# A fourth Strassen unit in token tile 2 of a pooled-attention and SiLU-MLP kernel, with VectorE and ScalarE work moved between tiles

## The chip, the cores and the metric

The kernel runs on one core of a Trainium2 chip. The metric is the device time of one execution in microseconds (us), lower is better. The kernel before takes 277.86 us, the median of 4 runs (277.79 to 278.11). In the profile's words, PE is TensorE (matmuls) and PEld its weight loads, DVE is VectorE, ACT is ScalarE, POOL is GpSimd, and SP is SyncE, which here only issues stores.

## The reference, cut to what matters

Eight batches of 576 tokens, eight heads of 64 features. Keys and values are averaged over groups of 8 tokens, so each head attends from 576 queries to 72 pooled keys. The result, 4608 tokens by 512 features, goes through a two-layer network with SiLU between. All arguments are float32; the kernel multiplies in bfloat16 and accumulates in float32.

```python
k_p = k.reshape(B, H, Sp, pool, D).mean(axis=3)
v_p = v.reshape(B, H, Sp, pool, D).mean(axis=3)
scores = scale * np.matmul(q, k_p.transpose(0, 1, 3, 2))
scores = scores - np.max(scores, axis=-1, keepdims=True)
attn = np.exp(scores)
attn = attn / (np.sum(attn, axis=-1, keepdims=True) + 1e-09)
x = (attn @ v_p), heads side by side      # [4608, 512]
h = x @ w_in                              # w_in [512, 2048]
g = h * (1.0 / (1.0 + np.exp(-h)))
out = (g @ w_out).astype(np.float32)      # w_out [2048, 512]
```

## The kernel before, in words

**Tiles.** The 4608 tokens are cut into nine token tiles of 512 (t = 0 to 8). A tile has an up stage (x @ w_in and SiLU, into the tile h_T, 16 groups of 128 hidden features) and a down stage (h_T @ w_out, into o_sb and out). While tile t runs, the attention of batch t + 1 is worked in between: q is transposed on VectorE (L164), scores go through exponentials on ScalarE (L353), denominators through a logarithm and an exponential (L372, L373), and numerators are scaled into xT on VectorE (L398). The batch is handled in three thirds, called visits. Pooling of k and v is done by accumulating DMAs from GpSimd's queue (L185, L189) and additions on GpSimd (L195, L198), from batch 3 on; batches 0 to 2 are pooled with VectorE sums (L268, L272).

**Units.** A plain group multiplies one group of 128 hidden features with four matmuls of 512 columns (L547). A unit is a 2 x 2 block product done with seven products in place of eight, after Strassen and Winograd. It covers four groups: seven products of four matmuls of 256 columns each (L493). The products need sums of input blocks (x_sum, L449, per tile) and sums of weight blocks (w_sum1, L442, made once), and their results are joined in PSUM and in the tiles r_sb, rr_sb, t_sb and c_sb (L511, L514, L517, L526, L529), with SiLU at L501. Units are named y = 0, 1, 2, 3, or A, B, C, E in a text program. The down stage is one such block product over the whole tile: seven products of 16 matmuls, from sums of hidden blocks (h_sum, L615, per tile) and of w_out blocks (w_sum, L633, made once).

**Which tile does what.** Tile 0 is all plain. Tile 1 has two units and eight plain groups, tile 2 three units and four plain groups, and tiles 3 to 8 four units. The constant `T4 = 3` says from which tile on `run(t)` is used. Before it, the up stage is a list of items, and every other engine's work is a filler with a step number in the lists f_up and f_down; the fillers are issued when the step is reached, so these numbers set the order in each engine's queue. The up stage of tile 1 has 60 steps, the down stage 112; fillers with larger numbers follow at the end. From T4 on the order is one text, PROGRAM, whose tokens name products (C2, E6), hidden sums (h5h), parts of the down products (d40), attention steps (sc0, de1, nu0), the next tile's input sums (x3) and two subtractions (u1, u2). All engines work in order.

**The down stage, two forms.** `down_quarters` (L656 to L690; tiles 1 and 2) issues the products 2, 5, 1, 4, 3, 7, 6. Products 5, 3 and 6 share the PSUM bank Q, and product 3's result is copied out of it to o_sb[0] at L682 before product 6 adds to it. `down_stages` (L712 to L754; from T4 on) begins with 4 and 3 and keeps their sum in rr_sb, from which two results are then subtracted at L754 (tokens u1, u2): on GpSimd for t below 7, on VectorE for tiles 7 and 8.

**Weight sums.** The sums of units 0 and 1 are made in tile 0, those of unit 2 at the end of tile 1 (into space that k and v of batch 2 leave), those of unit 3 at the end of tile 2: three into the same space and two into the tile w_e. The last halves of two w_out sums (n = 4 and 7) are made in the down stage of tile 1.

Of the kernel before, what the change touches and what calls it, by code (L numbers as in the profile page):

```python
# [36 lines left out]
def kernel(  # L37
# [9 lines left out]
    nc = tc.nc  # L47
# [594 lines left out]
    def down_quarters(t, fillers, last=False):  # L642
        step = spread(fillers, 7 * 2 * KQ)
        ps = {
            n: ps_tile([128, 2, CQ], FP32, "mm", f"o_ps{n}") for n in "PQR"
        }
        bank = {2: "P", 5: "Q", 1: "R", 4: "P", 3: "Q", 7: "P", 6: "Q"}
        begun = set()
        r_sb, rr_sb, t_sb = r_sbs[0], rr_sbs[0], t_sbs[0]

        def product(n, k0, k1, cs=(0, 1)):
            b = bank[n]
            for kt in range(k0, k1):
                for c in cs:
                    next(step)
                    nc.tensor.matmul(  # L656
                        ps[b][:, c, :], lhsT=left(n, kt, c), rhs=W_OUT[n][:, kt, :],
                        start=b not in begun,
                        stop=kt == k1 - 1, skip_group_check=True,
                    )  # L660
                    begun.add(b)

        add, sub = ALU.add, ALU.subtract
        tt = nc.vector.tensor_tensor
        KA = KQ // 2
        product(2, KA, KQ)
        product(5, KA, KQ)
        product(2, 0, KA)
        nc.scalar.copy(r_sb, ps["P"])
        product(5, 0, KA)  # L670
        tt(out=rr_sb, in0=ps["Q"], in1=r_sb, op=add)
        for cc in ((0,), (1,)) if last else ((0, 1),):
            cs = slice(cc[0], cc[-1] + 1)
            product(1, 0, KQ, cc)
            tt(out=t_sb[:, cs], in0=ps["R"][:, cs], in1=rr_sb[:, cs], op=sub)
            product(4, 0, KQ, cc)
            nc.scalar.copy(o_sb[1][:, cs, LO], ps["P"][:, cs])
            tail = last and cc == (1,)
            if tail:
                store(t, 3, LO, (nc.gpsimd,))  # L680
            product(3, 0, KQ, cc)
            nc.vector.tensor_copy(out=o_sb[0][:, cs, HI], in_=ps["Q"][:, cs])  # L682
            if tail:
                store(t, 1, HI)
            product(7, 0, KQ, cc)
            tt(out=o_sb[0][:, cs, LO], in0=ps["P"][:, cs], in1=t_sb[:, cs], op=add)
            for c in cc:
                store(t, c, LO if tail else FULL, (nc.scalar if tail else nc.sync,))
            product(6, 0, KQ, cc)
            tt(out=o_sb[1][:, cs, HI], in0=ps["Q"][:, cs], in1=t_sb[:, cs], op=add)  # L690
            for c in cc:
                if tail:
                    store(t, 3, HI, both)
                else:
                    store(t, 2 + c, FULL, (nc.gpsimd if last else nc.sync,))
        for _ in step:
            pass


    def down_stages(t, last):  # L700
        ps = {}
        bank = {2: "P", 5: "Q", 1: "R", 4: "P", 3: "Q", 7: "P", 6: "Q"}
        begun = set()
        r_sb, rr_sb, t_sb = r_sbs[0], rr_sbs[0], t_sbs[0]
        add, sub = ALU.add, ALU.subtract
        tt = nc.vector.tensor_tensor

        def matmuls(n, k0, k1, cs=(0, 1)):
            b = bank[n]
            for kt in range(k0, k1):  # L710
                for c in cs:
                    nc.tensor.matmul(  # L712
                        ps[b][:, c, :], lhsT=left(n, kt, c), rhs=W_OUT[n][:, kt, :],
                        start=b not in begun,
                        stop=kt == k1 - 1, skip_group_check=True,
                    )
                    begun.add(b)

        def after(n, cc=(0, 1), tail=False):
            cs = slice(cc[0], cc[-1] + 1)  # L720
            if n == 4:
                nc.scalar.copy(r_sb, ps["P"])
            elif n == 3:
                tt(out=rr_sb, in0=ps["Q"], in1=r_sb, op=add)
            elif n == 2:
                nc.scalar.copy(o_sb[1][:, :, LO], ps["P"])  # L726
                if last:
                    store(t, 3, LO, (nc.gpsimd,))
            elif n == 5:
                copy = nc.scalar.copy if last else nc.vector.tensor_copy  # L730
                copy(out=o_sb[0][:, :, HI], in_=ps["Q"])
                if last:
                    store(t, 1, HI)
            elif n == 1:
                tt(out=t_sb[:, cs], in0=ps["R"][:, cs], in1=rr_sb[:, cs], op=add)
            elif n == 7:
                tt(out=o_sb[0][:, cs, LO], in0=ps["P"][:, cs], in1=t_sb[:, cs], op=add)
                for c in cc:
                    store(t, c, LO if tail else FULL, (nc.scalar if tail else nc.sync,))
            else:  # L740
                tt(out=o_sb[1][:, cs, HI], in0=ps["Q"][:, cs], in1=t_sb[:, cs], op=add)
                for c in cc:
                    if tail:
                        store(t, 3, HI, both)
                    else:
                        store(t, 2 + c, FULL, (nc.gpsimd if last else nc.sync,))

        def part_of(tok):
            if tok == "o":
                return after(6)  # L750
            n = int(tok[1])
            if tok[0] == "u":
                src = o_sb[1][:, :, LO] if n == 1 else o_sb[0][:, :, HI]
                (nc.gpsimd if t < B - 1 else nc.vector).tensor_tensor(  # L754
                    out=rr_sb, in0=rr_sb, in1=src, op=sub
                )
                return
            b = bank[n]
            if b not in ps:
                tag = f"mm{'PQR'.index(b)}"  # L760
                ps[b] = ps_tile([128, 2, CQ], FP32, tag, f"o_ps{b}")
            i = int(tok[2])
            k0 = 2 * i if n == 4 else 2 * (i ^ 2)
            matmuls(n, k0, k0 + 2)
            if i == 3 and n != 6:
                after(n)

        def columns(c):
            if not c:
                ps["R"] = ps_tile([128, 2, CQ], FP32, "mm2", "o_psR")  # L770
            for n in (1, 7, 6):
                matmuls(n, 0, KQ, (c,))
                after(n, (c,), c == 1)

        return part_of, columns
# [163 lines left out]
    def load_half_2(name, half):  # L939
        for i0, i1 in ((0, SA), (SA, SLOTS), (SLOTS, SLOTS + 1)):  # L940
            load_slots(nc.gpsimd, 2, name, i0, i1, half)

    THREE = (
        "A2 A5 g0 B2 A4 A1 A3 B5 C2 A7 B4 A6 Ah B1 B3 As C5 B7 C4 B6 Bh C1 C3 C7 Bs g1"
        " C6 Ch Cs g2 g3",
        "A2 A5 g0 A4 B2 A3 A1 B5 A7 C2 A6 B4 B3 B1 C5 Ah B7 As C4 Bh B6 C1 C3 C7 Bs g1"
        " C6 Ch Cs g2 g3",
    )
    visits = [third(n) for n in range(3)]
    T4 = 3  # L950
    for t in range(NT):
        a = t + 1
        if t >= T4:
# [11 lines left out]
            f_up += [(17, lambda: numerators(0, part(1, 1)))]  # L965
        else:
            G = lambda *gs: [(g, 0, NTT) for g in gs]
            if t == 1:
                items = (
                    G(12, 13, 14, 15) + [(0, "25143"), (1, "2"), (0, "7"), (1, "5")]  # L970
                    + [(0, "6h"), (1, "1")] + G(0) + [(1, "4"), (0, "s"), (1, "3")] + G(1)
                    + [(1, "7h6")] + G(2) + [(1, "s")] + G(3)
                )
            else:
                items = []
                for it in THREE[t // B].split():
                    items += [(("BCA".index(it[0])), it[1])] if it[0] in "ABC" else G(int(it[1]))
            if t == 1:
                for n in U_X:
                    f_up.append((0, lambda n=n: unit_x_sum(t, n)))  # L980
# [1 line left out]
                h_at = 50 if t == B else 54 if t > 1 else 45  # L982
                f_up.append((h_at, lambda n=n: hidden_sum(n, 4, 8)))
            f_up.append((56, lambda: hidden_sum(6, 4, 8)))
            for n, k0 in ((2, 0), (5, 0), (1, 4), (1, 0)):
                f_up.append((64, lambda n=n, k0=k0: hidden_sum(n, k0, k0 + 4)))
            f_down.append((33 if t > 1 else 44, lambda: hidden_sum(7, 0, 8)))
            f_down.append((71 if t < B else 50, lambda: hidden_sum(6, 0, 4)))
# [1 line left out]
        for n, t0, f_to, at, parts in (  # L990
            (1, 0, f_down, 16, (0, 2)), (3, 0, f_down, 30, (0, 2)),
            (1, 0, f_down, 46, (2, PW)), (3, 0, f_down, 50, (2, PW)),
            (6, 0, f_down, 8, (0, PW)), (4, 0, f_down, 12, (0, 2)),
            (7, 0, f_down, 14, (0, 2)), (4, 1, f_down, 20, (2, PW)), (7, 1, f_down, 52, (2, PW)),
        ):
            for i in range(*parts):
                if t == t0:
# [64 lines left out]
        if t == 1:  # L1062
            def unit_weight_tiles():
                k_w = big.tile([128, 4, 2, 256], BF16, tag="k_raw2", name="w_sum12")
                v_w = big.tile([128, 4, 2, 256], BF16, tag="v_raw2", name="w_sum12")
                w_sum1.append([k_w[:, i] for i in range(4)] + [v_w[:, 0]])
                w_sum1.append([v_w[:, 1 + i] for i in range(3)] + [w_e[:, i] for i in range(2)])

            f_down.append((72, unit_weight_tiles))
            for i, n in enumerate(U_W):  # L1070
                f_down.append((73 if i < 2 else 81, lambda n=n: unit_weight_sum(2, n)))
        if t == 2:
            for i, n in enumerate(U_W):
                f_down.append((76 + 2 * i, lambda n=n: unit_weight_sum(3, n)))
        if t != 1:
            moe_tables()
        if t == 0:
# [34 lines left out]
```

The softmax here doesn't subtract the row's maximum and nothing guards it: scores larger than these inputs give would overflow.

## Time and profile before

| what | value |
|---|---|
| median of 4 runs | 277.86 us |
| the profiled execution, time | 277.86 us |
| its span, first to last instruction | 276.0 us |
| busy: PE, DVE, ACT, POOL | 269.9, 243.5, 192.4, 111.5 us |
| TensorE clock granted | 1.00 |
| h_sum, 128x1024 (L615), 76 of them | 788 ns mean |
| weight sum, 128x512 (L442, w_in) | 414 ns mean |
| copy of o_psQ at L682 on VectorE | 686 ns mean |
| copy of o_psP at L677 on ScalarE | 586 ns mean |
| subtraction at L754 on GpSimd, 8 of them; on VectorE, 4 | 1779 ns; 684 ns mean |
| first matmul of tiles 1, 2, 3, 4 | 50.91, 80.72, 109.45, 137.80 us |

The span is what the trace covers; the time of the execution holds 1.86 us more. A timeline row gives the start in us, the length, the engine, the line, what is written and read, and in brackets the idle time of that engine just before and what ended it. A run of equal instructions is merged into one row with a count. Two instructions of one engine overlap a little: a single input sum of 128x512 takes 0.42 us, but two take 0.75. A matmul's end is modelled, so the time of a matmul is best read from the start of one to the start of the next. A few matmul records are missing from the trace, and PE is then shown idle for that time.

### The profile page before, as it was taken

The numbers are of one execution on the slowest core, as the hardware profiler recorded it, in microseconds if no ns is written. First come the engines' busy times: TensorE is split into PE (matmuls) and PEld (weight loads), VectorE is DVE, ScalarE is ACT, GpSimd is POOL, SyncE is SP. The second block draws the span as 40 slices with busy tenths as digits, with TensorE's granted clock in tenths as the row PEclk, the third lists the DMA queues.
The fourth block names the chain that finished last, engine by engine and source line by source line (L and its number), as shares of the span: only waits on it lengthen the run. The fifth ranks groups of instructions, "written<-read, shape, count | busy, mean of one in ns | idle before, by whom it ended". The sixth has DMA issues, their size and how long they took to land.

```text
span 276.0 us, 7362 instructions
## 1 busy us (share of the span) xinstructions
PE 269.9 (98%) x2923; PEld 209.1 (76%) x2933; DVE 243.5 (88%) x452; ACT 192.4 (70%) x374; POOL 111.5 (40%) x112
## 2 busy tenths in 40 slices
PE   8999999999999999999999999999999999999995
PEld 4448444576778678887888778877887788888884
DVE  4986778778998879998999999999999899998994
ACT  1688767468668976789777986798688868407730
POOL 8755116342148530964377326986550400000000
PEclk9999999999999999999999999999999999999999
DMA  7999999997659879558846844599620042005003
GB/s 211 278 244 257 205 312 200 243 181 126 147 68 211 228 110 162 147 160 124 135 119 163 148 75 125 140 152 134 135 57 2 2 103 53 0 13 144 1 26 128
DMA packets 31314, 37.73 MB, mean 137 GB/s; under 512 B 10352, under 2 KB 22256, under 8 KB 31280
## 3 DMA queue, kind: packets, MB, share of 16 engines
q0 software_dynamic: 23920, 27.03, 52.3%
q1 hardware_dynamic: 6928, 9.58, 12.6%
q10 hardware_dynamic: 432, 0.66, 0.6%
q8 instruction: 23, 0.38, 0.6%
q14 instruction: 11, 0.09, 0.1%
HBM read 36.70 MB, written 9.44 MB: 167 GB/s over the span
## 4 chain that ended last, share of the span: by engine, by line
PE 83%; DMA 14%; issue 1%; POOL 0%; DVE 0%; POOLq 0%
PE u_psP L493 14%; PE u_psQ L493 14%; PE o_psQ L712 12%; PE o_psP L712 12%; DMA w_in_sb<-in_moe_w_in_dram 7%; DMA w_out_sb<-in_moe_w_out_dram 6%; PE u_psR L493 5%; PE o_psR L712 4%; PE o_psQ L656 4%; PE o_psP L656 4%; PE hp_ps L547 4%; PE sc_ps L345 3%; PE nu_ps L389 3%; PE o_ps L582 2%; DMA q_bf<-in_q_dram 2%; PE den_ps L363 2%
## 5 line engine op out<-in xcount | busy, mean ns | idle before, releaser
L615 DVE TENSOR_TENSOR h_sum<-h_T 128x1024 bf16<-128x1024 bf16 (+1 forms) x78 | 58.9, 799 | 2.8 <-ACT h_T L501 1.6
L493 PEld LDWEIGHTS <-w_sum 128*128 128x128 bf16 x532 | 52.0, 98 | 7.2 <-issue 0.3
L712 PEld LDWEIGHTS <-h_sum 128*128 128x128 bf16 x480 | 45.8, 98 | 8.1 <-issue 2.5
L353 ACT ACTIVATE es<-sc_ps 72x384 bf16<-72x384 f32 (+1 forms) x100 | 39.1, 472 | 5.5 <-PE sc_ps L345 5.3
L501 ACT ACTIVATE h_T<-c_sb 128x512 bf16<-128x512 f32 x58 | 35.7, 630 | 6.2 <-DVE c_sb L529 3.6
L511 ACT COPY r_sb<-u_psP 128x512 f32<-128x512 f32 x29 | 17.0, 586 | 19.3 <-PE u_psP L493 19.2
L547 PE MATMUL hp_ps<-xT,w_in_sb 128*128 128x512 bf16 (+2 forms) x151 | 26.1, 317 | 0.3
L398 DVE TENSOR_TENSOR xT<-nu_ps,rec 128x384 bf16<-128x384 f32 (+1 forms) x50 | 23.9, 528 | 1.8 <-PE nu_ps L389 1.4
L493 PEld LDWEIGHTS <-w_in_sb 128*128 128x128 bf16 x232 | 22.5, 98 | 2.9
L195 POOL TENSOR_TENSOR raw<-raw 72x1024 f32<-72x1024 f32 x10 | 23.7, 2367 | 0.1
L514 DVE TENSOR_TENSOR rr_sb<-u_psQ,r_sb 128x512 f32<-128x512 f32 x29 | 19.5, 682 | 3.6 <-PE u_psQ L493 1.9
L559 POOL DMA_DIRECT2D out_dram<-o_sb x2 | 1.2, 618 | 52.2 <-ACT o_sb L726 48.1
L553 ACT ACTIVATE h_T<-hp_ps 128x512 bf16<-128x512 f32 (+2 forms) x39 | 18.1, 477 | 5.8 <-PE hp_ps L547 4.8
L526 DVE TENSOR_TENSOR c_sb<-u_psP,t_sb 128x512 f32<-128x512 f32 x29 | 19.8, 681 | 2.0 <-PE u_psP L493 1.3
L547 PEld LDWEIGHTS <-w_in_sb 128*128 128x128 bf16 x156 | 14.6, 98 | 8.5 <-issue 0.8
L517 DVE TENSOR_TENSOR t_sb<-u_psR,rr_sb 128x512 f32<-128x512 f32 x29 | 19.6, 676 | 1.5 <-PE u_psR L493 0.5
L712 PEld LDWEIGHTS <-h_T 128*128 128x128 bf16 x192 | 18.5, 98 | 2.7
L529 DVE TENSOR_TENSOR c_sb<-u_psQ,t_sb 128x512 f32<-128x512 f32 x29 | 19.6, 675 | 1.0 <-PE u_psQ L493 0.8
L754 POOL TENSOR_TENSOR rr_sb<-rr_sb,o_sb 128x512 f32<-128x512 f32 x8 | 14.2, 1779 | 15.2 <-ACT o_sb L726 11.9
L501 ACT ACTIVATE h_T<-u_psP 128x512 bf16<-128x512 f32 x29 | 17.3, 598 | 3.3 <-PE u_psP L493 3.3
L501 ACT ACTIVATE h_T<-u_psQ 128x512 bf16<-128x512 f32 x29 | 17.3, 596 | 3.4 <-PE u_psQ L493 3.4
L372 ACT ACTIVATE lnd<-den_ps 128x384 f32<-128x384 f32 (+1 forms) x23 | 11.2, 487 | 11.2 <-PE den_ps L363 11.2
(106 smaller groups left out, 581.0 us busy)
## 6 DMA issues: line engine op xcount, KB each, us to landing
out_dram<-o_sb SPq DMA_DIRECT2D x128, 64.0 KB, 1.7
raw<-in_k_dram POOLq DMA_DIRECT2D x10, 576.0 KB, 7.7
raw<-in_v_dram POOLq DMA_DIRECT2D x10, 576.0 KB, 7.3
q_bf<-in_q_dram POOLq DMA_DIRECT2D x6, 576.0 KB, 10.1
w_in_sb<-in_moe_w_in_dram POOLq DMA_DIRECT2D x8, 256.0 KB, 8.6
w_out_sb<-in_moe_w_out_dram POOLq DMA_DIRECT2D x4, 512.0 KB, 13.5
raw<-in_v_dram POOLq DMA_DIRECT2D x2, 768.0 KB, 11.0
raw<-in_k_dram POOLq DMA_DIRECT2D x1, 768.0 KB, 10.4
```

The source lines that it names most:

```text
L195: nc.gpsimd.tensor_add(out=raw[:, :, : 2 * D], in0=raw[:, :, : 2 * D], in1=raw[:, :, 2 * D :])
L353: nc.scalar.activation(es[:, s, :], sc[s], func=AF.Exp, scale=score_scale)
L398: nc.vector.tensor_mul(out=xT[:, 2 * g0 + c : 2 * (g0 + ng - 1) + c + 1 : 2, cols], in0=nu[c][:, :w].rearrange("r (g n) -> r g n", g=ng), ...
L493: nc.tensor.matmul(ps[y, bank][:, u, :], lhsT=w[:, kk, 128 * u : 128 * (u + 1)], rhs=x[:, kk, :], start=first and u == 0 and kk == 0, stop ...
L501: nc.scalar.activation(h_T[:, g : g + 2, j * NQ : (j + 1) * NQ], src, func=AF.Silu)
L517: tt(out=t_sb, in0=ps[y, "R"], in1=rr_sb, op=ALU.subtract)
L526: tt(out=c_sb[0], in0=ps[y, "P"], in1=t_sb, op=ALU.add)
L529: tt(out=c_sb[1], in0=ps[y, "Q"], in1=t_sb, op=ALU.add)
L547: nc.tensor.matmul(hp_ps[:, r0:r1], lhsT=w_in_sb[:, kk, g * 128 : (g + 1) * 128], rhs=xT[:, kk, x0 : x0 + r1 - r0], start=(kk == 0), stop= ...
L615: nc.vector.tensor_tensor(out=h_sum[n][:, ks, :], in0=quarter(*a, ks), in1=quarter(*b, ks), op=op)
L656: nc.tensor.matmul(ps[b][:, c, :], lhsT=left(n, kt, c), rhs=W_OUT[n][:, kt, :], start=b not in begun, stop=kt == k1 - 1, skip_group_check= ...
L712: nc.tensor.matmul(ps[b][:, c, :], lhsT=left(n, kt, c), rhs=W_OUT[n][:, kt, :], start=b not in begun, stop=kt == k1 - 1, skip_group_check= ...
```

## The change

`T4` goes from 3 to 2, so tile 2 is worked by `run(2)`: four units, the joined text program, `down_stages`. For that, tile 1 makes the weight sums of the fourth unit as well: three behind those of the third unit (f_down step 84) and two in its up stage (f_up step 42). The last halves of the w_out sums 4 and 7 move from tile 1's down stage to the start of its up stage, and the upper half of hidden sum 1 from behind the up stage to step 57. The copy of product 3's result in `down_quarters`, which only tile 1 still uses, goes from VectorE to ScalarE. The subtractions u1 and u2 go to VectorE for tiles 5 and 6 as well, so GpSimd keeps those of tiles 2, 3 and 4. The other lines only remove what tile 2 no longer needs.

```diff
-            nc.vector.tensor_copy(out=o_sb[0][:, cs, HI], in_=ps["Q"][:, cs])
+            nc.scalar.copy(out=o_sb[0][:, cs, HI], in_=ps["Q"][:, cs])
...
-                (nc.gpsimd if t < B - 1 else nc.vector).tensor_tensor(
+                (nc.gpsimd if t < B - 3 else nc.vector).tensor_tensor(
...
-    T4 = 3
+    T4 = 2
...
-            if t == 1:
+            if True:
                 items = (
...
-            else:
-                items = []
-                for it in THREE[t // B].split():
-                    items += [(("BCA".index(it[0])), it[1])] if it[0] in "ABC" else G(int(it[1]))
...
             f_up.append((56, lambda: hidden_sum(6, 4, 8)))
-            for n, k0 in ((2, 0), (5, 0), (1, 4), (1, 0)):
+            f_up.append((57, lambda: hidden_sum(1, 4, 8)))
+            for n, k0 in ((2, 0), (5, 0), (1, 0)):
                 f_up.append((64, lambda n=n, k0=k0: hidden_sum(n, k0, k0 + 4)))
...
-            (7, 0, f_down, 14, (0, 2)), (4, 1, f_down, 20, (2, PW)), (7, 1, f_down, 52, (2, PW)),
+            (7, 0, f_down, 14, (0, 2)), (4, 1, f_up, 8, (2, PW)), (7, 1, f_up, 10, (2, PW)),
...
-                w_sum1.append([k_w[:, i] for i in range(4)] + [v_w[:, 0]])
-                w_sum1.append([v_w[:, 1 + i] for i in range(3)] + [w_e[:, i] for i in range(2)])
-
+                w_sum1[2] = [k_w[:, i] for i in range(4)] + [v_w[:, 0]]
+                w_sum1[3][:3] = [v_w[:, 1 + i] for i in range(3)]
+
+            w_sum1.extend(([], [None] * 3 + [w_e[:, i] for i in range(2)]))
             f_down.append((72, unit_weight_tiles))
             for i, n in enumerate(U_W):
                 f_down.append((73 if i < 2 else 81, lambda n=n: unit_weight_sum(2, n)))
-        if t == 2:
-            for i, n in enumerate(U_W):
-                f_down.append((76 + 2 * i, lambda n=n: unit_weight_sum(3, n)))
+                f_to, at = (f_down, 84) if i < 3 else (f_up, 42)
+                f_to.append((at, lambda n=n: unit_weight_sum(3, n)))
```

More of the change, by code (lines that the diff above doesn't have):

```diff
@@ L941, in load_half_2 @@
             load_slots(nc.gpsimd, 2, name, i0, i1, half)
[L943 to L948, printed above, removed]
     visits = [third(n) for n in range(3)]
-    T4 = 3
+    T4 = 2
     for t in range(NT):
```

## The prediction

> **What bounds the kernel now.** I read the page first: engine shares and the chain that ended last.
>
> ```profile
> PE 269.9 (98%) x2923; PEld 209.1 (76%) x2933; DVE 243.5 (88%) x452; ACT 192.4 (70%) x374; POOL 111.5 (40%) x112
> ...
> PE 83%; DMA 14%; issue 1%; POOL 0%; DVE 0%; POOLq 0%
> ```
>
> TensorE is 98% of the span and 83% of the chain; the DMA share lies in the start (weights arriving before 46 us), which the change leaves alone. A share of the span is an average, so I cut the span at the first matmul of each token tile and asked for busy time by stretch. These three rows are tiles 1, 2 and 3 (columns: length, then busy time and count of PE, PEld, DVE, ACT, POOL, then clock, DMA share, GB/s):
>
> ```profile
> 50.91:80.72 29.81, 29.70 (x328) 21.53 (x329) 25.96 (x57) 21.03 (x41) 9.15 (x9) 1.00 0.71 147
> 80.72:109.45 28.73, 28.62 (x324) 22.62 (x324) 24.80 (x47) 22.34 (x43) 12.68 (x10) 1.00 0.91 178
> 109.45:137.80 28.35, 28.35 (x339) 23.87 (x336) 26.51 (x48) 23.30 (x44) 16.04 (x12) 1.00 0.70 139
> ```
>
> PE fills each tile at a granted clock of 1.00. Tiles 4 and 5, which run the same program as tile 3, last 28.34 and 28.35 us. So a tile with the four-unit program costs 28.35, whatever the other engines do around it, and tile 2, with three units and four plain groups, costs 0.38 more. In the timeline of PE from 50 to 223 us I find one real wait: 0.17 us at 62.21, before product 6 of tile 1's second unit. The rest are pauses of about 0.09 us at each switch between 128-row and narrow attention matmuls, and single missing records. Only two things can move the end: the matmul time of tile 2, and a new wait of PE.
>
> **Part 1: tile 2 gets the fourth unit.** Removed: four plain groups, 16 matmuls of 512 columns. Added: one unit, 28 matmuls of 256 columns. Both prices stand in PE's timeline:
>
> ```profile
> 91.74 1.89 PE L547 MATMUL hp_ps<-xT,w_in_sb 128*128 128x512 bf16 x8
> ...
> 109.45 0.60 PE L493 MATMUL u_psP<-xT,w_sum 128*128 128x256 bf16 x4
> ...
> 112.51 0.60 PE L493 MATMUL u_psP<-x_sum,w_in_sb 128*128 128x256 bf16 x4
> ```
>
> The next piece starts at 93.47, so eight plain matmuls take 1.73 us (0.216 each) and sixteen 3.46. From 109.45 to 112.51 lie seven products: 3.06. The difference is -0.40. Whole tiles say 28.35 - 28.73 = -0.38; the missing 0.02 is a different number of switches. I take **-0.38**.
>
> A rule speaks against this step. The Trainium skill, "TensorE: Matmul & The Clock Gate", section "Back-to-back issue gap", gives a sustained roofline of about 81 ns per matmul of 128 columns and 131 ns at 512 in streams of weight load and matmul; read off linearly between them, 256 columns would be an estimated 98 ns. By it the swap would be 28 x 98 against 16 x 131, an estimated 0.65 us slower. The rows above have 216 ns and 109 ns in such streams, so this trace contradicts those two figures, and the sum goes by the rows.
>
> Tile 2 then has tile 3's engine load. Its start is alike, relative to the first matmul: VectorE's last transposed-input sums begin at -0.64 us in both tiles (80.08, 108.81), the last output sum at +1.03 and +1.04 (81.75, 110.49), the first residue copy on ScalarE at +0.68 and +0.69. The accumulator that the first new unit needs at its sixth product, +2.18 (5 x 0.437), is that of tile 1's last output sum, free at 82.43, or +1.71: cover 0.47. No term.
>
> **Part 2: work pulled into tile 1 on VectorE.** Its gaps there, in its timeline (start, length, what, idle before):
>
> ```profile
> 55.67 0.69 DVE L514 TENSOR_TENSOR rr_sb<-u_psQ,r_sb 128x512 f32<-128x512 f32 x1 [1.75 <-ACT r_sb L511]
> ...
> 61.87 1.29 DVE L615 TENSOR_TENSOR h_sum<-h_T 128x1024 bf16<-128x1024 bf16 x2 [0.81 <-ACT h_T L501]
> ...
> 65.95 2.50 DVE L615 TENSOR_TENSOR h_sum<-h_T 128x1024 bf16<-128x1024 bf16 x4 [0.99 <-ACT h_T L553]
> ...
> 76.79 0.68 DVE L682 COPY o_sb<-o_psQ 128x512 f32<-128x512 f32 x1
> ```
>
> - Four output-weight sums go ahead of the row at 55.67. In a run such sums take 0.75 for two, 0.34 each after the first: 1.42 in a gap of 1.75. Hidden, 0.3 spare; without the gap, 1.42 before rr_sb.
> - Two sums for w_e go ahead of the row at 61.87: 0.75 in 0.81. Hidden by 0.06; an overrun delays hidden sums whose product starts at 64.54, not PE.
> - One hidden sum moves from the four at 65.95 into the gap of 0.99: 0.60. Hidden, and the rest end 0.6 sooner.
> - From 65.95 on, 0.6 (hidden sum), 2 x 0.67 (output-weight sums gone) and 0.6 (copy gone) leave; three sums for the fourth unit come, 1.0. Two waits stop the early part of this gain from carrying through: the pooled v on PE (70.97) and t_sb on o_psR (71.73). From there I get t_sb at 72.9 (before 73.32), xT at 73.5, the hidden sum at 74.5, the eight weight sums from 75.1 to 77.8; the next output sum waits for PE until 78.5 as before (78.52). Cover 0.7.
>
> Added 8 sums plus a moved one, and every one lies in idle time: **0**, with bounds: below zero excluded by PE waiting for none of them; above, see rival A.
>
> **Part 3: the copy on ScalarE.** It moves from VectorE at 76.79 to behind four exponentials. The bank it empties is written again by product 6 on PE:
>
> ```profile
> 76.16 1.62 ACT L353 ACTIVATE es<-sc_ps 72x384 bf16<-72x384 f32 x4 [1.18 <-PE sc_ps L345]
> ...
> 78.26 0.38 PE L656 MATMUL o_psQ<-w_sum,h_sum 128*128 128x256 bf16 x2
> ```
>
> A copy behind such a group starts 1.50 after the group (97.16 after 95.66), here 77.66; the same copy at L677 takes 0.59: done 78.25. PE resumed 0.05 after the ScalarE read at 62.33, so 78.30 against 78.26: a wait of 0.04. Ends: 0 if the copy follows sooner; 0.16 if it starts only when the group ends (77.78 + 0.59 + 0.05). I take **+0.05**, nearest to the first of these rows. Behind the copy on ScalarE is the logarithm at 79.05, idle 1.27 before it: not reached. The store of these rows waits for a later sum at 78.52, so SP's order and times stay.
>
> **Part 4: subtractions.** Tile 2 gets two on GpSimd (tile 3: 1.80 and 1.58 us), queued behind the accumulating v load, with the next q load behind them:
>
> ```profile
> 99.23 1.39 POOL L189 DMA_DIRECT2D raw<-in_v_dram  x1 [4.70 <-issue]
> ...
> 128.94 1.80 POOL L754 TENSOR_TENSOR rr_sb<-rr_sb,o_sb 128x512 f32<-128x512 f32 x1 [0.97 <-ACT o_sb L726]
> ```
>
> GpSimd is free at 100.6; in tile 3's pace the first operand is there at +19.5, 100.2. So the first subtraction starts about 0.4 late and the second ends near 105.0. The q load behind them leaves some 4.5 us later (100.07 before), with 10.1 us to landing near 115, and is used in tile 4, after 137. Tiles 5 and 6 trade two subtractions on GpSimd for 2 x 0.68 on VectorE (tile 7's row). In tile 5 six hidden sums beside GpSimd's took 3.70 + 2.82 us against 3.69 for six in tile 8 without it: VectorE gives 1.4 and gains 2.8. In tile 6 one fits the idle 1.25 before the copy at 215.90, and the other replaces a lengthening (2.35 against 1.28 in tile 7). PE waits for neither now: **0**.
>
> **Sum.** 276.0 - 0.38 + 0.05 = 275.67 us. The profiled execution took 277.86, 1.86 outside the span, and equals the median of the four runs: 277.53, **277.5 us**. That is -0.12%; a measurement of this kernel tells about 0.2% (0.56 us) from no change, so this counts as the same.
>
> **Rivals.**
> - *A: the gain is eaten at the end of tile 1.* If GpSimd's load issues (76.72 to 78.85) slow the eight weight sums as its additions slow a hidden sum (1.18 at 147.57 against 0.68), eight cost 0.5 x 8 = 4 at worst; the covers of 0.7 and 0.47 go first, so it decides from 1.2 us of delay. Against it: in tile 3 four hidden sums beside a load issue (126.59) took 2.49, as in tile 6. A delay of 1.4, or the copy's 0.16 with some of it, gives about +0.3: **277.8**.
> - *B, slower: the subtractions of tile 2 come late.* VectorE runs in order, so t_sb waiting for the second holds the attention products and the sums that tile 3's fifth product (+1.75) reads. Tile 5 bore t_sb at +24.9 with about 0.1 to spare, so it decides when t_sb is past +25.0, 105.7: when GpSimd gets to the first subtraction after 101.6 instead of 100.6. The first half of v landed 6.6 after issue here; the longest in the trace is 8.7. That 2.1 less 1.0 of margin is +1.1: **278.6**. Against it: issue times and traffic ahead of this load are those of before.
> - *C: more is saved.* If the copy costs nothing and the wait of 0.17 at 62.21 vanishes: 276.0 - 0.38 - 0.17 + 1.86 = **277.3**. Against it: that wait is for ScalarE, whose order there is unchanged.
> - *D: the change doesn't do its swap* (tile 2 stays at 28.73): 277.9. The engines' instruction order shows the fourth unit in tile 2, so this has no chance of its own.
>
> **Numbers.** Forecast 0.70, A 0.13, B 0.08, C 0.09. Faster by over 0.2% means below 277.30: half of C and the low tail of the forecast, since runs spread by 0.3 us, 0.10. Slower, above 278.42: B, 0.08. The same: 0.82. The range 277.2 to 278.1 holds forecast, A and C with that scatter and leaves out B.
>
> **What would show it.** Right: tile 2 lasts 28.35, from first matmul to first matmul; tile 1 29.81 to 29.9; tiles 3 to 6 as now; PE's product 6 at the end of tile 1 starts at most 0.1 later; t_sb of tile 5 about 1 us sooner. Wrong: a gap on PE in tile 2 or at the first products of tile 3 (B), or at tile 2's sixth product (A).

## The result, and the profile after

The changed kernel took 277.43 us (median of 35 runs, 277.07 to 278.42) and the kernel before, run beside it, 278.02 us (56 runs, 277.39 to 278.84). The ratio is 0.9982 with a 95% interval of 0.9976 to 0.9987: 0.18% or 0.50 us less, at the edge of what can be told from no change. The two medians themselves lie 0.59 apart. The prediction was 277.5 us. Its profiled execution took 277.36 us with a span of 275.6.

These two lines of the changed kernel's page answer to the first two shown of before: busy time, share of the span and count of each engine, and the chain that ended last.

```profile
PE 270.2 (98%) x2937; PEld 210.8 (76%) x2945; DVE 249.0 (90%) x460; ACT 193.1 (70%) x376; POOL 107.7 (39%) x110
...
PE 95%; DVE 2%; ACT 1%; issue 1%; DVEq 0%
```

VectorE has eight instructions more, GpSimd two less. The DMA share of before lay in the start, which the change leaves alone, and here the chain runs back through TensorE instead. The entry to look at is DVE 2%, some 5 us: a stretch in which VectorE, not TensorE, set the pace. The cut at the first matmuls of tiles 1, 2, 3 and 4 says where (columns as in the prediction: length, then PE, PEld, DVE, ACT, POOL, clock, DMA share, GB/s).

```profile
50.54:80.39 29.85, 29.74 (x327) 21.53 (x328) 27.16 (x61) 21.51 (x42) 9.19 (x9) 1.00 0.73 149
80.39:108.74 28.35, 28.35 (x339) 23.88 (x336) 27.83 (x46) 23.33 (x44) 15.53 (x12) 1.00 0.84 166
108.74:137.41 28.67, 28.55 (x338) 23.79 (x336) 28.28 (x49) 22.68 (x43) 16.04 (x12) 1.00 0.75 145
```

Tile 1 is 0.04 longer than before (29.81), tile 2 is 0.38 shorter (28.73). But tile 3, whose program is untouched, is 0.32 longer than its 28.35. So this one execution won nearly nothing in these three tiles: that it is 0.50 below the profiled execution of before comes from tile 1 beginning 0.37 earlier (50.54 against 50.91) and from 0.10 less outside the span. Yet the medians too differ by 0.59, and no single profile explains a median. Both had to be explained.

First tile 3. Three cuts of the changed kernel's timeline: VectorE at the end of tile 2, GpSimd over the same time, and TensorE's weight loads at the start of tile 3 (start, length, engine, line, operation; idle time before in brackets).

```profile
98.36 4.47 DVE L615 TENSOR_TENSOR h_sum<-h_T 128x1024 bf16<-128x1024 bf16 x4
102.76 0.68 DVE L731 COPY o_sb<-o_psQ 128x512 f32<-128x512 f32 x1
103.36 2.36 DVE L615 TENSOR_TENSOR h_sum<-h_T 128x1024 bf16<-128x1024 bf16 x2
105.64 0.68 DVE L735 TENSOR_TENSOR t_sb<-o_psR,rr_sb 128x512 f32<-128x512 f32 x1
```

```profile
99.59 1.39 POOL L189 DMA_DIRECT2D raw<-in_v_dram  x1 [5.44 <-issue]
100.45 1.83 POOL L754 TENSOR_TENSOR rr_sb<-rr_sb,o_sb 128x512 f32<-128x512 f32 x1
103.58 1.59 POOL L754 TENSOR_TENSOR rr_sb<-rr_sb,o_sb 128x512 f32<-128x512 f32 x1 [1.30 <-DVE o_sb L731]
```

```profile
110.76 0.33 PEld L493 LDWEIGHTS <-w_in_sb 128*128 128x128 bf16 x4 [0.39 <-DVE x_sum L449]
```

The first subtraction came near its forecast: 20.06 us after the tile's first matmul, where the prediction had 19.9. That is luck in part: the prediction had GpSimd busy with the v load's issue for its whole 1.39 us, while here the subtraction starts 0.86 after that issue begins; but the issue itself came later in its tile, at +19.20 against +18.51 before. The surprise is elsewhere: four hidden sums took 4.47 us in place of some 2.5, and two took 2.36 in place of 1.28. The group's own row tells that one sum is stretched and not all:

```profile
L615 DVE TENSOR_TENSOR h_sum<-h_T x6: 674/678/2672, 98.4 to 104.0; 128x1024 bf16<-128x1024 bf16 x6
```

That is minimum, median and maximum in ns of six. The longest ended at 102.83, 0.56 after GpSimd's subtraction (100.45 + 1.83). So the copy behind it on VectorE came at 102.76, the second subtraction, which waits for that copy, at 103.58, and a second sum was held until it ended. t_sb started at 105.64, +25.25 from the tile's first matmul. Everything behind it on VectorE up to the input sums followed late, and tile 3's fifth product started 0.28 late.

### The profile page after: what moved, and what is told of

It is laid out like the page before. It is cut to its first block, busy times and chain, and to the rows that moved or that the text cites. A ratio compares the mean times of both kernels' runs of the same rounds, so it can differ in the third digit from the quotient of the medians.

```text
span 275.6 us, 7406 instructions
## 1 busy us (share of the span) xinstructions
PE 270.2 (98%) x2937; PEld 210.8 (76%) x2945; DVE 249.0 (90%) x460; ACT 193.1 (70%) x376; POOL 107.7 (39%) x110
## 4 chain that ended last, share of the span: by engine, by line
PE 95%; DVE 2%; ACT 1%; issue 1%; DVEq 0%
PE u_psP L493 14%; PE u_psQ L493 14%; PE o_psQ L712 13%; PE o_psP L712 13%; PE hp_ps L547 7%; PE o_ps L582 5%; PE u_psR L493 5%; PE o_psR L712 5%; PE sc_ps L345 4%; PE nu_ps L389 3%; PE warm_ps L851 3%; PE den_ps L363 2%; PE o_psQ L656 2%; PE o_psP L656 2%; PE warm_ps L855 1%
## 5 line engine op out<-in xcount | busy, mean ns | idle before, releaser
L615 DVE TENSOR_TENSOR h_sum<-h_T 128x1024 bf16<-128x1024 bf16 x79 | 60.7, 812 | 1.5 <-ACT h_T L501 0.9
L712 PEld LDWEIGHTS <-h_sum 128*128 128x128 bf16 x560 | 53.4, 98 | 9.5 <-issue 3.1
L493 PEld LDWEIGHTS <-w_sum 128*128 128x128 bf16 x544 | 53.1, 98 | 6.9 <-issue 0.3
L501 ACT ACTIVATE h_T<-c_sb 128x512 bf16<-128x512 f32 x60 | 36.8, 630 | 7.7 <-DVE c_sb L529 4.3
L493 PEld LDWEIGHTS <-w_in_sb 128*128 128x128 bf16 x240 | 23.3, 98 | 3.4 <-DVE x_sum L449 0.4
L712 PEld LDWEIGHTS <-h_T 128*128 128x128 bf16 x224 | 21.5, 98 | 3.2
L547 PE MATMUL hp_ps<-xT,w_in_sb 128*128 128x512 bf16 (+2 forms) x137 | 22.4, 311 | 0.2
L553 ACT ACTIVATE h_T<-hp_ps 128x512 bf16<-128x512 f32 (+2 forms) x35 | 15.9, 464 | 5.1 <-PE hp_ps L547 4.1
L547 PEld LDWEIGHTS <-w_in_sb 128*128 128x128 bf16 x140 | 13.0, 98 | 7.2 <-issue 0.8
L493 PE MATMUL u_psP<-x_sum,w_in_sb 128*128 128x256 bf16 x120 | 18.2, 273 | 0.1
L493 PE MATMUL u_psP<-xT,w_sum 128*128 128x256 bf16 x120 | 18.0, 273 | 0.0
```

The source lines that it names most:

```text
L493: nc.tensor.matmul(ps[y, bank][:, u, :], lhsT=w[:, kk, 128 * u : 128 * (u + 1)], rhs=x[:, kk, :], start=first and u == 0 and kk == 0, stop ...
L501: nc.scalar.activation(h_T[:, g : g + 2, j * NQ : (j + 1) * NQ], src, func=AF.Silu)
L547: nc.tensor.matmul(hp_ps[:, r0:r1], lhsT=w_in_sb[:, kk, g * 128 : (g + 1) * 128], rhs=xT[:, kk, x0 : x0 + r1 - r0], start=(kk == 0), stop= ...
L615: nc.vector.tensor_tensor(out=h_sum[n][:, ks, :], in0=quarter(*a, ks), in1=quarter(*b, ks), op=op)
L712: nc.tensor.matmul(ps[b][:, c, :], lhsT=left(n, kt, c), rhs=W_OUT[n][:, kt, :], start=b not in begun, stop=kt == k1 - 1, skip_group_check= ...
```

## The experiments

Theory: GpSimd's subtractions hold hidden sums up; this makes t_sb late; TensorE waits at the next tile's fifth product when t_sb is past about +24.9; and in tile 5 of the kernel before, the same wait stood at its edge, so the change removes it there and may bring it in tile 2. Rivals: the v load is late (the prediction's rival B), or the gain lies elsewhere. All ratios are to the kernel before, run beside. Edits are to the changed kernel unless it says otherwise.

**The changed kernel again**, unedited.

> The changed kernel once more, nothing edited. In its first profile tile 0 ended 0.37 us sooner than before (first matmul of tile 1 at 50.54 against 50.91), tile 1 was 0.04 longer, tile 2 0.38 shorter and tile 3 0.32 longer (two waits of TensorE, 0.28 before the fifth product and 0.05 before the seventh). Theory scatter: tile 0's end moves by some tenths from run to run in both kernels and is no effect of the change; tile 1 stays at 29.85, tile 2 at 28.35, and tile 3 between 28.35 and 28.7, since its wait hangs on when a DMA lands. Rival: tile 0 ends near 50.5 again, by something in the new program. Time by both: 277.4 to 277.5, ratio near 0.998.

277.55 us, before 278.37, ratio 0.9977 (0.9966 to 0.9988). In this profile tile 3 lasts 28.34: no wait. Tile 2 began 0.45 us later than in the first profile (80.84), and GpSimd's v load and subtraction stood at nearly the same absolute times (99.42, 100.33). The longest hidden sum took 2.05 us, t_sb came at +24.62. So the wait is not a fixed cost of the change: it depends on how GpSimd falls against the tile. What moves GpSimd is a load, as the expectation said. The v load adds its second half to the first, so its issue waits until the first half has landed, and that took 7.3 us from issue in the first profile and 6.7 here. (In tile 2 of all 14 profiles the v load's issue starts 1.1 us after this landing, whatever its row's bracket names.) GpSimd in this profile, for comparison with the rows above:

```profile
99.42 1.39 POOL L189 DMA_DIRECT2D raw<-in_v_dram  x1 [3.15 <-DVE rr_sb L724]
100.33 1.77 POOL L754 TENSOR_TENSOR rr_sb<-rr_sb,o_sb 128x512 f32<-128x512 f32 x1
```

From tile 2's first matmul the load's issue stands at +18.58 and the subtraction at +19.49, where the first profile has +19.20 and +20.06.

**The kernel before again**, unedited.

> The kernel before once more, nothing edited, for a second profile. Theory scatter: the first matmul of tile 1 lies somewhere from 50.4 to 51.2, tiles 1, 2 and 3 last 29.81, 28.73 and 28.35 as before. Rival (tile 0 differs by program): 50.9 again.

One execution, 278.15 us. Now tile 6 of the kernel *before* lasts 29.43 in place of 28.88, with t_sb of tile 5 at +25.45. Its timelines, VectorE at the end of tile 5, GpSimd, and TensorE at the start of tile 6:

```profile
183.81 4.27 DVE L615 TENSOR_TENSOR h_sum<-h_T 128x1024 bf16<-128x1024 bf16 x4
...
191.36 0.68 DVE L735 TENSOR_TENSOR t_sb<-o_psR,rr_sb 128x512 f32<-128x512 f32 x1
```

```profile
186.28 4.61 POOL L754 TENSOR_TENSOR rr_sb<-rr_sb,o_sb 128x512 f32<-128x512 f32 x2
```

```profile
196.49 0.61 PE L493 MATMUL u_psP<-x_sum,w_in_sb 128*128 128x256 bf16 x4 [0.32 <-DVE x_sum L449]
```

It is much the same picture, in the place where the change takes the subtractions away from GpSimd. The profile on which the prediction was built had t_sb there at +24.89 and no wait:

```profile
191.04 0.68 DVE L735 TENSOR_TENSOR t_sb<-o_psR,rr_sb 128x512 f32<-128x512 f32 x1
```

Two things differ from tile 2. The v load's issue is longer (185.41 to 187.38), the first subtraction, begun beside it, takes 2.92 us in place of 1.6 to 1.8, and the first held sum ends 1.10 before that subtraction does, so what ended this hold isn't shown. And the second subtraction follows the first with a gap of only 0.08, so the load and the long first subtraction set its end, 190.89. t_sb reads its result and starts 0.47 after that, when the held hidden sum ahead of it in VectorE's queue is done.

**Tile 2's subtractions on VectorE.**

```diff
-                (nc.gpsimd if t < B - 3 else nc.vector).tensor_tensor(
+                (nc.gpsimd if 2 < t < B - 3 else nc.vector).tensor_tensor(
```

> The changed kernel with tile 2's two subtractions on VectorE as well. Theory port (a subtraction on GpSimd holds up a hidden sum on VectorE until it ends: one took 2.67 us in place of 0.68, and everything behind it up to tile 3's input sums came late): the hidden sum takes 0.68, t_sb of tile 2 comes at about +24.3 after the tile's first matmul instead of +25.25, tile 3 lasts 28.35, and the time falls by 0.3 against the changed kernel, to 277.1. Rival late load (the subtraction is late because the v load ahead of it on GpSimd is): the same 277.1. Rival input sums (tile 3 waits for something else than the subtractions): tile 3 stays at 28.67, 277.4.

In tile 2 the four sums now take 2.48 and t_sb starts 0.1 after the second subtraction ends on VectorE, at +24.01, though VectorE does two instructions more:

```profile
98.36 2.48 DVE L615 TENSOR_TENSOR h_sum<-h_T 128x1024 bf16<-128x1024 bf16 x4
...
104.41 0.69 DVE L735 TENSOR_TENSOR t_sb<-o_psR,rr_sb 128x512 f32<-128x512 f32 x1
```

Tiles 2 and 3 last 28.34 each. And the load was as late as in the first profile of the changed kernel: the first half of v landed after 7.4 us, and the issue that waited for it stands at 99.67, +19.28:

```profile
99.67 1.39 POOL L189 DMA_DIRECT2D raw<-in_v_dram  x1 [5.41 <-issue]
```

So a late load alone makes no wait. The profile agrees with the theory. The time does not: 277.87 us, ratio 0.9983 (0.9974 to 0.9992), no better than the changed kernel. The span's median over the timed runs is 275.70, against 275.75 for the changed kernel beside it; what lies outside the span is 2.09 us against 1.79. That part was not expected; the last section comes back to it.

**The same, and an operation on GpSimd that nobody needs.** Its result is not used.

```diff
+                if t == 2:
+                    nc.gpsimd.tensor_tensor(out=rr_sbs[1], in0=src, in1=src, op=sub)
```

> Tile 2's two subtractions on VectorE, and in their place on GpSimd two operations of the same shape that read the same results and whose output nobody uses. Theory port: the hidden sum is held up all the same (about 2.7 us), VectorE has 1.2 us more to do, t_sb of tile 2 comes at +25.3 or later, and tile 3 waits 0.3 to 1.5 us: 277.4 to 278.6. Rival late load: nobody waits for GpSimd's result, so no wait in tile 3, 277.1.

The wait is back, with nothing depending on GpSimd's result. GpSimd at the end of tile 2, and TensorE at the start of tile 3:

```profile
99.97 1.51 POOL L758 TENSOR_TENSOR rr_sb<-o_sb 128x512 f32<-128x512 f32 x1
103.38 1.35 POOL L758 TENSOR_TENSOR rr_sb<-o_sb 128x512 f32<-128x512 f32 x1 [1.90 <-DVE o_sb L731]
```

```profile
111.13 0.61 PE L493 MATMUL u_psP<-x_sum,w_in_sb 128*128 128x256 bf16 x4 [0.39 <-DVE x_sum L449]
```

Four sums took 3.57 and two 2.12, t_sb came at +25.51, tile 3 lasts 28.96. 278.13 us, 1.0000 (0.9988 to 1.0013). The v load's issue comes earlier here (99.02, +18.54) than in the kernel above, VectorE's work is the same in both, and nothing at the end of the tile waits for GpSimd's result. So a late load isn't needed either: GpSimd's own activity beside the hidden sums suffices, with the two subtractions in VectorE's queue. In the changed kernel itself, with its subtractions on GpSimd, the hold alone left t_sb below the limit, and hold and late load together passed it: its three profiles have t_sb at +24.40, +24.62 and +25.25 where the first half of v landed after 6.5, 6.7 and 7.3 us.

**The change of tiles 5 and 6 alone**, put into the kernel before:

```diff
-                (nc.gpsimd if t < B - 1 else nc.vector).tensor_tensor(
+                (nc.gpsimd if t < B - 3 else nc.vector).tensor_tensor(
```

> The kernel before with one edit: the subtractions of tiles 5 and 6 on VectorE. The prediction's step (part 4) gave this 0. Theory port: in the second profile of the kernel before, the same subtractions on GpSimd held up a hidden sum of tile 5 for 2.47 us, t_sb came at +25.4 and tile 6 waited 0.55 us; in the first, t_sb at +24.9 just bore it. With them on VectorE t_sb of tile 5 comes at +24.0 in every run, tile 6 lasts 28.88 always, and the median falls by 0.2 to 0.5 us, ratio 0.998 to 0.9993. Rival (tile 5's wait was one odd run): ratio 1.0, the median within 0.1 of the kernel before.

277.70 us, before 278.28, 0.9978 (0.9966 to 0.9991): an edit that the prediction booked at nothing makes the kernel faster by itself, by an interval that leaves out 1. Tile 6 lasts 28.88, t_sb of tile 5 stands at +24.01. The v load's issue stands beside the four hidden sums of tile 5 as before, and they take 2.48 us in all: that issue alone holds none of them.

**All but that**: the changed kernel with the subtractions of tiles 5 and 6 on GpSimd again (`t < B - 1` in the same line).

> The changed kernel with the subtractions of tiles 5 and 6 back on GpSimd. Theory port: tile 5's t_sb at +24.9 to +25.4 and tile 6 at 28.88 to 29.43 again, tile 3 as in the changed kernel (28.35 to 28.7); the gain left is the unit's 0.38 less 0.04 and less tile 3's wait: ratio 0.9985 to 1.0. Rival: ratio 0.998 as the changed kernel.

277.99 us, 0.9990 (0.9974 to 1.0005). Tile 2 lasts 28.34; tile 6 lasts 29.21, with t_sb of tile 5 at +25.23. The wait of before is back.

**The unit without the moves**: copy on VectorE, hidden sum 1 and the halves of sums 4 and 7 in their old places, all five weight sums of the fourth unit in the down stage, subtractions of tiles 5 and 6 on GpSimd.

```diff
-            nc.scalar.copy(out=o_sb[0][:, cs, HI], in_=ps["Q"][:, cs])
+            nc.vector.tensor_copy(out=o_sb[0][:, cs, HI], in_=ps["Q"][:, cs])
...
-            (7, 0, f_down, 14, (0, 2)), (4, 1, f_up, 8, (2, PW)), (7, 1, f_up, 10, (2, PW)),
+            (7, 0, f_down, 14, (0, 2)), (4, 1, f_down, 20, (2, PW)), (7, 1, f_down, 52, (2, PW)),
...
-                f_to, at = (f_down, 84) if i < 3 else (f_up, 42)
-                f_to.append((at, lambda n=n: unit_weight_sum(3, n)))
+                f_down.append((84, lambda n=n: unit_weight_sum(3, n)))
```

> The kernel before with the fourth unit in tile 2 and no more: its five weight sums stand at the end of tile 1 behind those of the third unit, nothing is moved into tile 1's gaps, the copy stays on VectorE and the subtractions of tiles 2 to 6 on GpSimd. The prediction's step (part 2) says that the moves lie in idle time and the cover is 0.7 and 0.47: without them VectorE runs the weight sums until about 80.1 in place of 77.8, the output sum that frees a bank ends at about 84.0, and tile 2's sixth product, due 2.18 after its first, waits about 1.1 us. Tile 2 29.4 to 29.5, time 0.6 to 0.9 above the kernel before, ratio 1.002 to 1.003. Rival: VectorE's cover is larger than read and tile 2 lasts 28.35, ratio 0.9987.

279.17 us, 1.0033 (1.0018 to 1.0047): slower than before. Tile 2 lasts 29.61, 1.27 over 28.34. Its output sum comes at 79.98, and TensorE's seventh product waits until the bank that it writes has been read (0.48 us of the 1.27 were lost already at the second product, which waits for xT); the delay goes on through t_sb, and tile 3 lasts 28.79:

```profile
84.51 0.60 PE L493 MATMUL u_psQ<-x_sum,w_in_sb 128*128 128x256 bf16 x4 [0.64 <-DVE rr_sb L514]
```

**The moves without the unit**, put into the kernel before: `T4 = 3` stays, tile 1 has the copy on ScalarE and the pulled work.

```diff
-            nc.vector.tensor_copy(out=o_sb[0][:, cs, HI], in_=ps["Q"][:, cs])
+            (nc.scalar.copy if t == 1 else nc.vector.tensor_copy)(
+                out=o_sb[0][:, cs, HI], in_=ps["Q"][:, cs]
+            )
```

> The kernel before with tile 1's moves and no fourth unit in tile 2: the same VectorE order in tile 1 as in the changed kernel, the copy on ScalarE in tile 1 alone, tile 2 with three units and plain groups as before, subtractions as before. By the prediction's parts 2 and 3: tile 1 29.85 (0.04 for the copy), tile 2 28.73, the rest as before; ratio 1.0 within 0.0007. Rival: the added VectorE work costs TensorE something in tile 1 that the fourth unit hid: tile 1 over 29.9.

278.49 us, 1.0006 (0.9993 to 1.0020). Tile 1 lasts 29.85 and tile 2 28.74: the moves cost 0.04 and bring nothing by themselves. Tile 6 shows the wait again (29.30, t_sb of tile 5 at +25.32).

**The copy back on VectorE**, all else as changed (the first lines of the diff of the unit without the moves).

> The changed kernel with the copy of product 3's result in tile 1 back on VectorE. By the prediction's part 3 the copy on ScalarE costs TensorE 0.04: tile 1 lasts 29.81 in place of 29.85. On VectorE the copy takes 0.6 of the cover of 0.7 behind the eight weight sums, so the output sum behind them still starts when TensorE lets it, and tile 2 lasts 28.35. Time 0.04 below the changed kernel, which the runs can't tell. Rival (VectorE needs the room): the output sum starts late, and tile 2's sixth product waits some tenths.

277.92 us, 0.9991 (0.9978 to 1.0003). Tile 1 regains its 0.04, but tile 2 lasts 28.87. The rival in the expectation holds, and I had expected the other: VectorE at the end of tile 1 and the start of tile 2, then TensorE.

```profile
76.47 0.69 DVE L682 COPY o_sb<-o_psQ 128x512 f32<-128x512 f32 x1 [0.86 <-PE o_psQ L656]
77.08 2.09 DVE L442 TENSOR_TENSOR w_sum<-w_in_sb 128x512 bf16<-128x512 bf16 x6
79.08 0.68 DVE L686 TENSOR_TENSOR o_sb<-o_psP,t_sb 128x512 f32<-128x512 f32 x1
...
82.89 1.27 DVE L514 TENSOR_TENSOR rr_sb<-u_psQ,r_sb 128x512 f32<-128x512 f32 x2
```

```profile
83.62 0.60 PE L493 MATMUL u_psQ<-x_sum,w_in_sb 128*128 128x256 bf16 x4 [0.36 <-DVE rr_sb L514]
```

The copy on VectorE is more than its 0.69: in the order of the changed kernel VectorE is so far ahead there that it idles 0.86 for TensorE to finish the bank, and six weight sums stand behind it. The output sum comes at 79.08 in place of 78.15, rr_sb at 82.89 in place of 82.02 (0.12 of each is tile 1's later start), and the seventh product is 0.53 late.

**Both: tile 2's subtractions and the copy on VectorE**, and **all subtractions and the copy on VectorE** (`nc.vector.tensor_tensor(` for every tile).

> The changed kernel with tile 2's two subtractions and tile 1's copy on VectorE; GpSimd keeps the subtractions of tiles 3 and 4. Theory port: t_sb of tiles 2, 5 and 6 at +24.0, of tiles 3 and 4 at +24.3, all below the limit of +24.9, tile 1 29.81, tiles 2 to 5 28.35, tile 6 28.88, in every run. Against the kernel before this is the unit's 0.38 and tile 6's wait, 0.3 in the mean: ratio 0.9975. Rival: no better than the changed kernel, 0.998.

> All subtractions and the copy on VectorE, GpSimd with none. Theory port: no hidden sum of the tiles 2 to 6 behind a subtraction is held up, t_sb at +24.0 in all of them, tile lengths as with tile 2's alone, since tiles 3 and 4 made nobody wait: ratio 0.9975. Rival: VectorE's 2.7 us more in tiles 3 and 4 cost something there: tiles over 28.35.

278.23 us, 1.0000 (0.9990 to 1.0011), and 278.13 us, 1.0006 (0.9994 to 1.0018). Both expectations failed, for the two reasons above: tile 2 lasts 28.87 in both because of the copy, and 2.13 us lie outside the span. That VectorE's order has no wait left at tiles 3 and 6 (28.35, 28.88) does not make up for it.

**The changed kernel beside these three.**

> The changed kernel once more beside these, unedited. Tile 1 29.85, tile 2 28.35, tile 3 28.35 or up to 28.7 with t_sb of tile 2 past +24.9, tile 6 28.88: ratio 0.998.

277.57 us, before 278.11, 0.9979 (0.9966 to 0.9991); t_sb of tile 2 at +24.40, tile 3 28.35. None of the versions tried is faster than the changed kernel.

## Why the prediction was right, and where it was not

The time was right, and part of the reason was not. Some of it is luck: the prediction set out 0.16 too low (277.86 against 278.02) and put the gain 0.26 too small (0.33 against 0.59 between the medians), and the two errors work against each other. The steps in turn:

- **Part 1, -0.38.** Tile 2 went from 28.73 to 28.35, and to 28.34 in other profiles. Here mechanism and size are right.
- **Part 2, 0.** No wait of TensorE at the work pulled into tile 1. The eight weight sums end in time; the output sum behind them follows an idle time of 0.65, where the prediction had a cover of 0.7. But the second cover, 0.47 at tile 2's sixth product, was taken at the wrong place. The seventh product is the tight one: an output sum 0.81 late (measured from tile 1's first matmul, copy on VectorE) cost 0.53 and one 1.56 late (unit without the moves) cost 1.27, a cover of 0.28 and 0.29. So rival A decides from 0.9 us of delay and not from 1.2.
- **Part 3, +0.05.** Measured +0.04 (29.81 to 29.85, in all profiles with the copy there). ScalarE and TensorE of the changed kernel show the reckoning line by line:

```profile
77.30 0.59 ACT L682 COPY o_sb<-o_psQ 128x512 f32<-128x512 f32 x1
```

```profile
77.94 0.38 PE L656 MATMUL o_psQ<-w_sum,h_sum 128*128 128x256 bf16 x2
```

  The copy starts 1.50 after its group of exponentials (75.80) and ends at 77.89, and product 6 follows 0.05 later. What the step did not price is the other side: the same copy left on VectorE would have cost 0.53 in tile 2. The prediction counted its going as 0.6 of relief that only adds to a cover; in fact the gain of part 1 hangs on it.
- **Part 4, 0.** This is the step that failed. "PE waits for neither now: 0" was read off one execution, and for tile 5 that execution stood right at the limit (t_sb at +24.89). In the five profiles that have subtractions on GpSimd in tile 5, the wait in tile 6 is 0, 0.55, 0.33, 0.23 and 0.42 us, 0.31 in the mean; on VectorE it is 0 in all nine. In tile 2 the three profiles of the changed kernel have 0.34, 0 and 0, 0.11 in the mean (and 0 with all subtractions on GpSimd). So the two halves of part 4 are about -0.31 and +0.11, not 0 and 0. What the step left out is the lengthening of hidden sums beside GpSimd as a delay of t_sb, and that the margin changes from one execution to the next with the landing of a load.
- **The limit** of +25.0 for t_sb in rival B was good: where t_sb is at most +24.89 there is no wait, and at +25.13, +25.23, +25.25, +25.32, +25.45 and +25.51 the next tile is 0.23, 0.33, 0.34, 0.42, 0.55 and 0.62 us late, each the excess over +24.9 within 0.02. In five more tiles t_sb stands at +25.02 to +26.62, but those had lost 0.34 to 1.27 us at their own start; counted after that loss, four lie below +24.7 and make no wait, and the fifth, at +25.35, makes one of 0.45.
- **Its route** was half right. A load was late in the profile with the wait, as B has it (7.3 us to landing, where the prediction took 6.6). But with the subtractions on VectorE a load as late did no harm. What B lacked is that GpSimd's operation holds a VectorE instruction that does not touch its data. B allowed 4.1 us from the start of the first subtraction to t_sb (101.6 to 105.7); the three profiles of the changed kernel have 5.19, 5.13 and 4.92. So the margin of 1.0 that B set against a late load did not exist: a subtraction at +19.9, the prediction's own forecast, already puts t_sb at about the limit. In tile 5 both act too: in all five profiles with subtractions on GpSimd the first one starts 0.86 or 0.87 after the v load's issue does, between +19.82 and +20.75, and t_sb starts 0.47 after the second one ends. The prediction had the sign of the hold in hand (six sums took 6.52 us beside GpSimd and 3.69 without) and used it only to say that tile 5 would gain time.
- **Rivals A, C and D** did not come. Tile 1 is longer by the copy's 0.04 alone, so nothing was lost at its end beyond that and nothing more was saved; tile 2 has the 339 matmul records of the four-unit program.

The sum with the measured sizes is -0.38 + 0.04 - 0.31 + 0.11 = -0.54 us; the runs give -0.50 by the ratio and -0.59 by the medians. The forecast's -0.33 was set against an execution of 277.86, which had no wait in tile 6. The size of the two halves of part 4 rests on few profiles, though, and the timed runs alone don't separate it from that of the unit: the edit of tiles 5 and 6 alone gave 0.9978, and all the rest 0.9990, each with some 0.0013 to 0.0015 either way.

The Trainium skill, "SBUF — State Buffer", section "Who interferes with whom", has a rule for this: a VectorE instruction with two SBUF inputs contends with a GpSimd instruction that reads SBUF. Of the pair of ports that the two engines share it says that it is an exclusive lock, and, beside another kind of VectorE instruction, that whoever issues first has it for the whole instruction and the other is fully blocked. The hidden sum has two such inputs, and in tile 2 its lengthening from 0.68 to 2.67 us, ended 0.56 after GpSimd's operation, agrees with a full block. On the order the trace agrees less: this sum has a recorded start of 100.16, 0.29 before the subtraction's 100.45, and was the one held. Tile 5 of the kernel before agrees less too, as said: a held sum ended 1.10 before the subtraction. That the lock is the cause is the page's account; the runs show the hold and what it costs. The rule spoke against giving tile 2 subtractions on GpSimd, and weighing it in part 4 would have pointed at the half of the route that rival B lacked.

## What to carry to other kernels

One profile shows waits, not margins: an edge with 0.0 to spare in the profiled execution was a wait in the four other profiles here, as a load landed sooner or later, so work out for each hand-over by how much it is early, and book a change that moves off such an edge as a gain. Take a second profile of the kernel before, where it is to be had, ahead of calling an edit free. When an instruction is moved off a busy in-order engine, price also what was queued behind it and what it would have waited for there; and work moved to GpSimd beside such sums of two SBUF tiles on VectorE was not free for VectorE here, even when nothing waited for GpSimd's result.

## What the runs showed that was not expected

- **VectorE held by GpSimd.** A hidden sum of 0.68 us took 2.67, 2.05 and 1.77 us beside GpSimd operations of 1.83, 1.77 and 1.51 us; the operation whose result is not used did it as well.
- **A step outside the span.** The time of an execution less its span has medians of 1.76 to 1.80 us in every timed kernel with at most 461 VectorE instructions on its page (451, 452, 456, 457, 460 and 461), and 2.09, 2.14, 2.13 and 2.13 us in those with 462, 462, 463 and 467. It is 0.3 us that no view of the trace shows, and it eats what tile 2's subtractions on VectorE save. Whether it is the count is open: all four kernels also have those subtractions on VectorE, and no run takes the two apart. A kernel with them there, the copy on ScalarE, and fewer VectorE instructions elsewhere was not tried.
- **The start scatters.** The first matmul of tile 1 stood between 50.44 and 52.16 us in 14 profiles, with the same program ahead of it. Such a spread is larger than the whole effect, so tiles were compared from first matmul to first matmul and not by absolute times.
